# Fewer VectorE operations for products and weighted values, and input rows in the value projections' tile

## The chip, the cores and the metric

The kernel runs on one core of a Trainium2 chip. The metric is the device time of one execution in microseconds. The core's engines are TensorE (PE in the profile, its weight loads PEld), VectorE (DVE), ScalarE (ACT), GpSimd (POOL) and SyncE (SP). POOL and SP also issue DMA transfers.

## The reference

Two branches read the same input `x` of 2048 rows and 640 columns, and a gate mixes them:

```python
g = _sigmoid((x * gate_w).sum(-1, keepdims=True))
a = _A_ref(x, A_wqkv, A_wo)        # 32 heads of 20, each row looks at 8 rows, 2 apart
b = _B_ref(x, B_A_re, ..., B_Dskip)
return g * a + (1 - g) * b

# A: sliding dilated attention
logits = jnp.einsum("bhsd,bhswd->bhsw", q, kg) * scale      # kg, vg: rows s, s-2, ..., s-14
attn = _softmax(logits, axis=-1)
o = jnp.einsum("bhsw,bhswd->bhsd", attn, vg)                # then o @ wo

# B: state space convolution
P = jnp.exp(logdA[:, :, None] * l[None, None, :])           # 640 x 192 x 2048, complex
K = jnp.einsum("dn,dnl,dn->dl", Cc, P, dB).real
y = irfft(rfft(u) * rfft(K))[:L] + u * Dskip
```

## The kernel before

The program has a main stage and a tail. The main stage runs the attention and builds the convolution kernel `K` side by side; the tail does the convolution in the frequency domain, mixes and stores. In each stage, the work is a list of named tasks with an engine each. The order of the tasks is a table of numbers (`ORDER`), and every engine executes its tasks strictly in that order. A task that waits holds back everything behind it on its engine.

**Attention.** The projections of q, k and v (L284) are computed in four pieces of 512 rows into PSUM tiles `tb`, of which there are two, and copied out by ACT or DVE into `qr`, `kr` and, for v, into the tile `prj`. `prj` holds all four pieces of v. Each finished piece is stored to DRAM (`vS`, L313), and for each of eight blocks of 256 rows a window of it is loaded back as `vc` (L337), two loads per block into two buffers in turn. Per block, DVE forms the products `prod` of q and shifted k (L343, five operations), TensorE sums them over a head (`lg`), DVE takes the maxima (`mx`, `hi`, `lo`), TensorE subtracts them, ACT takes the exponentials, and the probabilities pass through DRAM to `asb`. Then DVE multiplies the windows of v with them (`pv`, L417, five operations of 128x2048 a block), TensorE sums (`tb`, L424), and the output projection follows (L448).

**Convolution kernel.** `K` is built in ten chunks of three units. For a unit, ACT writes sines (L784, `trg`) and exponentials (L786, `exq`) into rings of slots in the tiles `big` and `bufA`. A slot has 32 groups; a group of `trg` has 32 sines and twice 21 sines, and a group of `exq` has 32 and 21 exponentials. DVE multiplies them in three operations (L806 twice with 1024 elements, the second with the sines read backwards, and L808 with 1344) into `pt` and `qq`, and TensorE contracts these in 64 or 128 small matrix products (L824, `kps`). The tasks are `pq`, `pqb`, `pqc` (DVE) and `kmm{chunk}{unit}{0..3}` (TensorE).

**Input rows.** The convolution needs `x` in another layout, `Usb` (128 x 64 x 160). It is loaded in eight pieces (`rows0` to `rows7`, L972) by POOL into the memory of `prj`, as a new tile in the same place, so the first load waits for the last store of `prj`. Ahead of each later piece, POOL copies two elements of the one before (`pace`, L971), which makes POOL wait until that piece has landed. `Usb` is read by the matrix products of L1276 at the end of the main stage.

## Time and profile before

| | |
|---|---|
| median of three runs | 325.98 us (324.89 to 327.3) |
| profiled execution | 324.97 us, its span 323.2 us |
| DVE busy | 294.0 us, 91% of the span, 408 instructions |
| ACT busy | 281.5 us, 87% |
| PE busy | 278.4 us, 86% |
| POOL busy | 62.8 us, 19% |
| chain that ended last | PE 48%, ACT 39%, issue 5%, DVE 3% |
| tail (from about 254 us) | about 69 us |

A busy share says how much an engine did, not who held up whom. The chain of waits is followed back from the last instruction; it says which work the end actually hung on. Both are read together with the table of idle times and what ended them.

### The profile page before, as it was taken

To read this page: it belongs to the slowest core of one execution; us is meant where nothing else is said; L and a number is where in the kernel's file an instruction comes from. 1 tells how busy PE (TensorE), PEld (TensorE's weight loads), DVE (VectorE), ACT (ScalarE), POOL (GpSimd) and SP (SyncE) were. 2 spreads that over 40 slices of the span, in tenths; PEclk is the share of its full clock that TensorE was granted. 3 is DMA by queue.
4 is the path that set the end of the run, shared out by engine and by line. 5 is a ranking of instruction groups with operands and counts; after the bars stand their busy time and mean duration, and the time that the engine had idled before them with its cause. 6 is when DMAs were issued, how large, how long until landed. Compare 5 with 4: busy or idle time off the path is not lost.

```text
span 323.2 us, 11733 instructions
## 1 busy us (share of the span) xinstructions
PE 278.4 (86%) x5109; PEld 170.3 (53%) x5134; DVE 294.0 (91%) x408; ACT 281.5 (87%) x425; POOL 62.8 (19%) x94
## 2 busy tenths in 40 slices
PE   0599997999979999999998979889999999997750
PEld 0145543444545645546554545457678776657740
DVE  4888999899998999999999989898998999999891
ACT  1479678999989999999999999899988599996991
POOL 8500026501100000111134523320200000000063
PEclk9999999999999999999999997999999999997995
DMA  8997356662414102467774996533860593962057
GB/s 213 338 227 224 122 173 138 130 128 83 92 30 109 37 6 74 81 161 254 179 190 97 161 179 141 108 96 77 254 258 33 151 312 95 204 123 44 2 135 194
DMA packets 48697, 45.65 MB, mean 141 GB/s; under 512 B 28590, under 2 KB 42482, under 8 KB 48646
## 3 DMA queue, kind: packets, MB, share of 16 engines
q1 hardware_dynamic: 42524, 27.82, 33.7%
q0 software_dynamic: 5216, 16.39, 20.8%
q8 instruction: 40, 0.66, 0.9%
q10 hardware_dynamic: 906, 0.69, 0.7%
q14 instruction: 11, 0.09, 0.1%
HBM read 28.25 MB, written 14.01 MB: 131 GB/s over the span
## 4 chain that ended last, share of the span: by engine, by line
PE 48%; ACT 39%; issue 5%; DVE 3%; SPq 2%; DMA 2%; POOL 0%; POOLq 0%; ACTq 0%; DVEq 0%
PE tb L284 14%; ACT big L784 8%; PE fp L1043 7%; PE ar L769 7%; ACT big L786 6%; PE kps L824 5%; ACT bufA L476 4%; PE tb L424 4%; PE tb L448 4%; ACT L160 3%; PE bp L1276 3%; ACT tt L1140 2%; ACT bufA L784 2%; ACT sp_k L476 2%; DMA bufA<-in_A_wqkv_dram 2%
## 5 line engine op out<-in xcount | busy, mean ns | idle before, releaser
L284 PE MATMUL tb<-bufA 128*128 128x512 bf16 x275 | 73.4, 394 | 6.5 <-DMA bufA<-in_A_wqkv_dram 2.9
L784 ACT ACTIVATE big<-ar 128x740 bf16<-128x740 int16 (+1 forms) x72 | 56.1, 849 | 2.4 <-PE ar L769 1.9
L786 ACT ACTIVATE big<-ar 128x848 bf16<-128x848 f32 x60 | 50.4, 919 | 3.2 <-PE ar L769 3.0
L769 PE MATMUL ar<-Rarg,L 64*128 64x212 bf16 (+4 forms) x600 | 47.1, 253 | 6.3 <-ACT big L784 2.5
L284 PEld LDWEIGHTS <-bufA 128*128 128x128 bf16 x300 | 32.3, 121 | 35.2 <-issue 12.0
L417 DVE TENSOR_TENSOR pv<-vc,asb 128x2048 bf16<-128x2048 bf16 x40 | 47.6, 1217 | 1.1 <-DMA vc<-vS 0.9
L343 DVE TENSOR_TENSOR prod<-qr,kr 128x2048 bf16<-128x2048 bf16 x40 | 47.8, 1218 | 0.5 <-PE lg L349 0.5
L769 PEld LDWEIGHTS <-L 64*128 64x128 bf16 x600 | 22.3, 95 | 35.0 <-issue 32.1
L806 DVE TENSOR_TENSOR pt<-big 128x1024 bf16<-128x1024 bf16 x48 | 32.1, 701 | 1.5 <-PE kps L824 0.8
L824 PE MATMUL kps<-qq,pt 128*32 128x21 bf16 (+1 forms) x2560 | 28.1, 175 | 3.3 <-issue 3.1
L824 PEld LDWEIGHTS <-pt 128*32 128x32 bf16 (+1 forms) x2560 | 23.4, 91 | 12.2 <-issue 10.1
L448 PE MATMUL tb<-wo_sb,oTm 128*128 128x320 bf16 x160 | 27.1, 300 | 0.1
L337 POOL DMA_DIRECT2D vc<-vS x16 | 11.5, 727 | 70.6 <-DVE pv L417 65.4
L476 ACT ACTIVATE sp_u<-fp 128x640 bf16<-128x640 f32 x29 | 22.4, 883 | 2.1 <-PE fp L1043 2.1
L476 ACT ACTIVATE sp_k<-fp 128x640 bf16<-128x640 f32 x30 | 22.7, 878 | 1.0 <-PE fp L1043 0.8
L424 PE MATMUL tb<-pv,ind 128*64 128x512 bf16 (+1 forms) x192 | 22.7, 359 | 0.3 <-ACT qr L476 0.2
L808 DVE TENSOR_TENSOR qq<-big 128x1344 bf16<-128x1344 bf16 x24 | 21.2, 884 | 0.0
L1043 PEld LDWEIGHTS <-PHI 128*128 128x128 bf16 x160 | 15.6, 97 | 8.1 <-issue 1.5
L1161 POOL DMA_DIRECT2D out_dram<-ot x14 | 7.8, 562 | 54.9 <-DVE ot L1143 54.9
L448 PEld LDWEIGHTS <-oTm 128*128 128x128 bf16 x160 | 14.5, 98 | 7.3 <-issue 2.7
L160 ACT ACT_TABLE_LOAD x14 | 18.0, 1283 | 0.3
L476 ACT ACTIVATE qr<-tb 128x512 bf16<-128x512 f32 (+1 forms) x22 | 10.8, 514 | 6.7 <-PE tb L284 6.7
(153 smaller groups left out, 512.0 us busy)
## 6 DMA issues: line engine op xcount, KB each, us to landing
vc<-vS POOLq DMA_DIRECT2D x16, 327.5 KB, 5.8
vS<-prj POOLq DMA_DIRECT2D x4, 640.0 KB, 5.7
gaS<-ga SPq DMA_DIRECT2D x8, 320.0 KB
Usb<-in_A_x_dram POOLq DMA_DIRECT2D x8, 320.0 KB, 5.0
gaF<-gaS SPq DMA_DIRECT2D x8, 320.0 KB
bufA<-in_A_wqkv_dram SPq DMA_DIRECT2D x3, 800.0 KB
Sprm<-pc SPq DMA_DIRECT2D x10, 240.0 KB
L<-Sprm SPq DMA_DIRECT2D x38, 60.0 KB
```

The costliest lines, as they stand in the source:

```text
L284: nc.tensor.matmul(ppf, self.wq[:, which, kt, e::5], self.xT[:, c0 // 1024, kt, c0 % 1024:c0 % 1024 + SC], start=(kt == 0), stop=(kt == NK ...
L343: nc.vector.tensor_tensor(b[e][:], self.qr[:, sc % NRB, e, :].unsqueeze(1).to_broadcast([128, W, C]), win(self.kr[:, sc % NRB, e, :], 0, W ...
L417: nc.vector.tensor_tensor(o, vw, b["asb"][:].unsqueeze(2).to_broadcast(sh), ALU.mult)
L424: nc.tensor.matmul(b["op", e][64 * a:64 * a + 64, 0:n, :], ind[:, 32:96], b["pv", e][:, w, a, 0:n, :], start=(w == 0), stop=(w == 3), skip ...
L448: nc.tensor.matmul(apf[:, :320], b["oT"][:, e, i * 128:(i + 1) * 128], wo_sb[:, e, hf * 320:(hf + 1) * 320], start=(e == 0), stop=(e == 4))
L476: nc.scalar.activation(o, i, ACT.Identity)
L769: nc.tensor.matmul(ar[:, g2, a0:a0 + ncol], L[rows, gv, sb, l0:l0 + 128], R[rows, c0:c0 + ncol], start=True, stop=True, tile_position=(64 ...
L784: nc.scalar.activation(d_[:, :, s0 * QW:s1 * QW], ar[:].bitcast(I16)[:, :, 0:2 * (s1 - s0) * QW:2], ACT.Sin, scale=SCL)
L786: nc.scalar.activation(dst[:, gp::2].rearrange("p g s n -> p g (s n)"), ar[:, :, 0:2 * EW], ACT.Exp)
L806: nc.vector.tensor_tensor(pt[:, :, k, :], gg[:, :, ::-1] if k else gg, e1, ALU.mult)
L824: nc.tensor.matmul(kps[32 * g:32 * g + 32, h ^ (g // 2), NM * ql:NM * ql + NM], pt[rows, k, v, :], qq[rows, k, v, :], start=(g not in star ...
L1043: nc.tensor.matmul(fp[:, fl % 2, 0:320].rearrange("p (c x) -> p c x", x=32), phis[fb][:, fl, kind, :], B[:, :, 2 * f1 + ri].rearrange("p c ...
```

## The change

Three things are changed.

1. **Products.** The constant table behind the sines is laid out anew, so that a group of `trg` reads: 21 sines of the second kind reversed, 32 sines, 21 sines of the first kind. One slice of 53 sines, read forwards from element 21 or backwards from element 52, then meets the 53 exponentials of a group, and two operations of 32 x 53 elements write what `pt` and `qq` held, side by side in one tile `pq`. The task `pqc` is gone; `pq` and `pqb` are longer. TensorE reads its operands from `pq`.
2. **Weighted values.** `vS` is laid out as 64 x 5 x 2 x rows, so that the windows of four rows of v lie one after another in `vc`, and one operation of 128x4096 takes the place of two of 128x2048. A block has three operations instead of five. Each store of `prj` to `vS` becomes two stores.
3. **Input rows.** `Usb` is now a view of the tile `prj` itself. Pieces 0 to 3 lie where the first two pieces of v were, and follow the first two stores only; pieces 4 to 7 follow all stores. The copies `pace` are gone. Instead each load waits for a task of TensorE named in `TICKS`.

```diff
+TICKS = ("kmm120", "kmm220", "kmm320", "kmm420", "kmm600", "kmm620", "kmm710", "kmm720")
...
-    "560 -1 -541 1 28 1 1 163 -124 1 1 123 -152 1 140 -139 37D 114 1 1 -152 139 14 1 -153 1 186 2 -178 1 1 141 1 393 -559 "
+    "544 -1 -525 1 28 1 1 163 -124 1 1 123 -152 1 140 -139 37D 114 1 1 -152 139 14 1 -153 1 184 2 -176 1 1 141 1 374 -540 "
...
-        self.vS = dr.tile([128, 5, HALO + S], BF16, name="vS")
+        self.vS = dr.tile([64, 5, 2, HALO + S], BF16, name="vS")
...
             def store(_, c0=c0, sc=sc):
-                nc.gpsimd.dma_start(self.vS[:, :, HALO + c0:HALO + c0 + SC], open_()[:, sc])
+                for a in range(2):
+                    nc.gpsimd.dma_start(self.vS[:, :, a, HALO + c0:HALO + c0 + SC], open_()[a::2, sc])
...
-                    sh, step, o = ([128, 4, 2, C], VW, b["pv", e][:, :, k]) if n == 2 else ([128, 4, 2, C], 5 * VW, b["pv", e][:, :, :, 0])
-                    vw = bass.AP(vt[:].tensor, vt[:, k, e, :].offset, [list(vt[:].ap[0]), [DIL, 4], [step, 2], [1, C]])
-                    nc.vector.tensor_tensor(o, vw, b["asb"][:].unsqueeze(2).to_broadcast(sh), ALU.mult)
+                    vw = bass.AP(vt[:].tensor, vt[:, e, 0, :].offset, [list(vt[:].ap[0]), [DIL, 4], [VW, 2 * n], [1, C]])
+                    nc.vector.tensor_tensor(b["pv", e][:, :, 0:2 * n], vw, b["asb"][:].unsqueeze(2).to_broadcast([128, 4, 2 * n, C]), ALU.mult)
...
-    rr = np.concatenate([np.concatenate([p, q.reshape(64, 4, -1)], axis=2).reshape(64, -1) for p, q in ((sp, sq), (ep, eq))], axis=1)
+    rr = np.concatenate([np.concatenate([sq[:, :, 1, ::-1], sp, sq[:, :, 0]], axis=2).reshape(64, -1), np.concatenate([ep, eq], axis=2).reshape(64, -1)], axis=1)
...
-                        b["pq", u] = self.tb.tile([128, 32, 2, KI], BF16, name="pt"), self.tb.tile([128, 32, 2, NM], BF16, name="qq")
-                    pt, qq = b["pq", u]
-                    if k < 2:
-                        nc.vector.tensor_tensor(pt[:, :, k, :], gg[:, :, ::-1] if k else gg, e1, ALU.mult)
-                    else:
-                        nc.vector.tensor_tensor(qq[:], trg[:, :, KI:].rearrange("p a (v m) -> p a v m", v=2),
-                                                exq[:, :, KI:].unsqueeze(2).to_broadcast([128, 32, 2, NM]), ALU.mult)
+                        b["pq", u] = self.tb.tile([128, 32, 2, KI + NM], BF16, name="pq")
+                    nc.vector.tensor_tensor(b["pq", u][:, :, k, :], trg[:, :, KI + NM - 1::-1] if k else trg[:, :, NM:], exq, ALU.mult)
...
-                                                     pt[rows, k, v, :], qq[rows, k, v, :],
+                                                     pq[rows, k, v, 0:KI], pq[rows, k, v, KI:],
...
-        g, h = n // 2, n % 2
+        g, h = n % 4, n // 4
         if n == 0:
-            P["Usb"] = pre.tile([128, 64, 160], BF16, name="Usb", tag="uga")
-        else:
-            g0, h0 = (n - 1) // 2, (n - 1) % 2
-            nc.gpsimd.tensor_copy(P["pace"][32 * g0:32 * g0 + 32, :], P["Usb"][32 * g0:32 * g0 + 32, 32 * h0, 0:2])
+            P["Usb"] = P["prj"]()[:].rearrange("p a e s -> p (a e s)").rearrange("p (b d) -> p b d", d=160)
...
-            ub.append(pl.add(f"rows{n}", "G", 1.4 if n else 0.7, lambda _, n=n: rows(n), deps=ub[-1:], after=list(at.stored.values()), dma=2.0))
+        ticks = {t.name: t for t in pl.tasks}
+        for n, tick in enumerate(TICKS):
+            ub.append(pl.add(f"rows{n}", "G", 0.7, lambda _, n=n: rows(n), deps=[ticks[tick]], after=ub[-1:] + [v for k, v in at.stored.items() if k < 2 or n >= 4], dma=2.0))
+            ub[-1].waits = [ticks[tick]]
```

On PE, ACT and SP the tasks stand in the same order as before. On DVE the removed operations are left out and the others keep their order. On POOL the row loads move.

The first place is DVE where the first weighted values and the first units of products are made, at 60.8 to 72 us of the trace. `prod` and `pv` are the products of the attention, `mx`, `hi`, `lo` the maxima, `kr<-tb` the copy of a projection out of PSUM. Before:

```order
L806 TENSOR_TENSOR pt<-big 128x32x32 x2
L343 TENSOR_TENSOR prod<-qr,kr 128x2048
L808 TENSOR_TENSOR qq<-big 128x1344
L343 TENSOR_TENSOR prod<-qr,kr 128x2048 x2
L417 TENSOR_TENSOR pv<-vc,asb 128x4x512
L365 TENSOR_REDUCE mx<-lg 128x64
L368 TENSOR_SCALAR hi<-mx 128x64
L369 SCALAR_TENSOR_TENSOR lo<-mx,hi 128x64
L806 TENSOR_TENSOR pt<-big 128x32x32 x2
L478 CAST kr<-tb 128x2x256
L417 TENSOR_TENSOR pv<-vc,asb 128x4x512
L808 TENSOR_TENSOR qq<-big 128x1344
```

And now:

```order
L802 TENSOR_TENSOR pq<-big 128x32x53 x2
L345 TENSOR_TENSOR prod<-qr,kr 128x2048 x3
L418 TENSOR_TENSOR pv<-vc,asb 128x4096
L367 TENSOR_REDUCE mx<-lg 128x64
L370 TENSOR_SCALAR hi<-mx 128x64
L371 SCALAR_TENSOR_TENSOR lo<-mx,hi 128x64
L802 TENSOR_TENSOR pq<-big 128x32x53 x2
L477 CAST kr<-tb 128x2x256
```

The second `pv` and the `qq` that stood behind the copy `kr<-tb` are now done in the longer operations ahead of the maxima and of the copy.

The second place is POOL from the store of v's second piece to the window loads for blocks 4 to 6. `vS<-prj` is a store of v, `vc<-vS` the window loads (two per block), `Usb` and later `prj<-in_A_x_dram` the row loads, `Kx<-X` and `kc<-Kx` the convolution kernel on its way through DRAM. Before, up to the fourth row load:

```order
L313 DMA vS<-prj 640x1x512
L337 DMA vc<-vS 64x10x262 x4
L313 DMA vS<-prj 640x1x512
L898 DMA Kx<-X 64x4x640
L313 DMA vS<-prj 640x1x512
L972 DMA Usb<-in_A_x_dram 32x32x160
L907 DMA kc<-Kx 128x2560
L971 COPY pace<-Usb 32x2
```

And now, the whole stretch:

```order
L315 DMA vS<-prj 320x1x512 x2
L339 DMA vc<-vS 64x10x262 x2
L960 DMA prj<-in_A_x_dram 32x32x160 x3
L339 DMA vc<-vS 64x10x262 x2
L315 DMA vS<-prj 320x1x512 x2
L960 DMA prj<-in_A_x_dram 32x32x160
L890 DMA Kx<-X 64x4x640
L315 DMA vS<-prj 320x1x512 x2
L899 DMA kc<-Kx 128x2560
L960 DMA prj<-in_A_x_dram 32x32x160 x2
L339 DMA vc<-vS 64x10x262 x4
L960 DMA prj<-in_A_x_dram 32x32x160 x2
```

Four row loads now stand ahead of the last store of v. Two more stand ahead of the window loads for blocks 4 and 5, which before stood behind the fourth and the fifth row load and their copies.

## Prediction

> **What bounds the kernel now.** I read the page first: the busy times and the chain that ended last.

> ```profile
> span 323.2 us, 11733 instructions
> ```
> ```profile
> PE 278.4 (86%) x5109; PEld 170.3 (53%) x5134; DVE 294.0 (91%) x408; ACT 281.5 (87%) x425; POOL 62.8 (19%) x94
> ```
> ```profile
> PE 48%; ACT 39%; issue 5%; DVE 3%; SPq 2%; DMA 2%; POOL 0%; POOLq 0%; ACTq 0%; DVEq 0%
> PE tb L284 14%; ACT big L784 8%; PE fp L1043 7%; PE ar L769 7%; ACT big L786 6%; PE kps L824 5%; ACT bufA L476 4%; PE tb L424 4%; PE tb L448 4%; ACT L160 3%; PE bp L1276 3%; ACT tt L1140 2%; ACT bufA L784 2%; ACT sp_k L476 2%; DMA bufA<-in_A_wqkv_dram 2%
> ```

> DVE is the busiest engine, and the change takes work from it. Yet the chain runs over DVE for 3% of the span, some 9.7 us. Where those lie is told by the chain in order of time. It has eleven pieces on DVE; here are the first and the last:

> ```profile
> 247.54 0.56 DVE ga L459
> 314.75 1.07 DVE ot L1143 x2
> ```

> Ahead of 247.5 us the chain does not touch DVE at all, and `prod`, `pv` and the products of L806 and L808 all lie ahead of that. The busy times by stretch say who fills the main stage (from, to, length, then the busy us of PE, PEld, DVE, ACT and POOL with the number of instructions):

> ```profile
> 60.00:230.00 170.00, 157.16 (x3776) 90.77 (x3795) 161.98 (x231) 165.28 (x240) 30.71 (x42) 0.99 0.50 117
> 230.00:254.00 24.00, 23.57 (x191) 17.66 (x189) 22.39 (x25) 19.56 (x29) 2.18 (x4) 1.00 0.48 161
> ```

> From 60 to 230 us ACT works 165.28 of 170 us, 97%, against 95% for DVE and 92% for PE. From 230 to 254 us PE works 98%. Neither engine gets less work by the change. The longest entries of the table of idle times, ACT's and PE's for 60 to 230 us, then DVE's:

> ```profile
> ACT big L786 <- PE ar L769: 3.0, 3, 1.3
> ```
> ```profile
> PE kps L824 <- issue: 3.1, 4, 1.3
> ```
> ```profile
> DVE ga L459 <- PE tb L448: 1.2, 2, 1.0
> ```

> ACT waits for PE, PE for its own instructions, DVE for PE. DVE runs close behind no one: it is ahead and is waited for only in short spots. PE's weight loads name those:

> ```profile
> L824 PEld LDWEIGHTS <-pt 128*32 128x32 bf16 x1280 | 12.3, 93 | 5.8 <-issue 4.3 <-DVE prod L343 0.2 <-DVE pv L417 0.2
> L824 PEld LDWEIGHTS <-pt 64*32 64x32 bf16 x1280 | 11.1, 90 | 6.4 <-issue 5.9 <-DVE qq L808 0.2
> L424 PEld LDWEIGHTS <-ind 128*64 128x64 bf16 x192 | 9.6, 110 | 8.5 <-issue 4.3 <-DVE qq L808 0.2 <-DVE bufA L478 0.2
> ```

> Five times 0.2, that is 1.0 us, is all that DVE shows as a cause there.

> **Products.** The groups and two stretches of DVE's timeline:

> ```profile
> L417 DVE TENSOR_TENSOR pv<-vc,asb 128x2048 bf16<-128x2048 bf16 x40 | 47.6, 1217 | 1.1 <-DMA vc<-vS 0.9 <-PE tb L424 0.2
> L806 DVE TENSOR_TENSOR pt<-big 128x1024 bf16<-128x1024 bf16 x48 | 32.1, 701 | 1.5 <-PE kps L824 0.8 <-ACT big L784 0.4 <-ACT big L786 0.3
> L808 DVE TENSOR_TENSOR qq<-big 128x1344 bf16<-128x1344 bf16 x24 | 21.2, 884 | 0.0
> ```
> ```profile
> 60.83 1.32 DVE L806 TENSOR_TENSOR pt<-big 128x1024 bf16<-128x1024 bf16 x2
> 62.07 1.22 DVE L343 TENSOR_TENSOR prod<-qr,kr 128x2048 bf16<-128x2048 bf16 x1
> 63.21 0.88 DVE L808 TENSOR_TENSOR qq<-big 128x1344 bf16<-128x1344 bf16 x1
> 64.01 2.44 DVE L343 TENSOR_TENSOR prod<-qr,kr 128x2048 bf16<-128x2048 bf16 x2
> ```
> ```profile
> 66.37 1.22 DVE L417 TENSOR_TENSOR pv<-vc,asb 128x2048 bf16<-128x2048 bf16 x1
> 67.50 0.68 DVE L365 TENSOR_REDUCE mx<-lg 128x64 f32<-128x512 f32 x1
> ```

> Operations overlap by some 0.08 us, so I take the distance between starts. Two `pt` take 62.07 - 60.83 = 1.24, or 0.62 each for 1024 elements; `qq` takes 64.01 - 63.21 = 0.80 for 1344; `pv` takes 67.50 - 66.37 = 1.13 for 2048. A unit costs 1.24 + 0.80 = 2.04 us. From 1024 to 2048 elements the time grows by 0.51, 0.50 ns an element. A new operation has 32 x 53 = 1696 elements: from `pt` 0.62 + 672 x 0.0005 = 0.96, from `qq` 0.80 + 352 x 0.0005 = 0.98. I take 0.97, so 1.94 a unit, and 0.10 less than before. Bounds by proportion: from `pv` 1.13 x 1696/2048 = 0.94, from `qq` 0.80 x 1696/1344 = 1.01, a gain of 0.16 or 0.02 a unit. For ten chunks of three units: **3.0 us** of DVE (0.6 to 4.8). The elements are the same number; only one start per unit is saved.

> **Weighted values.** 4096 elements: twice 1.13 = 2.26 at most, 1.13 + 2048 x 0.0005 = 2.15 at least; I take the middle, 2.20. Sixteen pairs become one: 16 x 0.06 = **1.0 us** (0 to 1.8). With the products DVE loses 4.0 us of work (0.6 to 6.6).

> None of it lies on the chain. What it can reach is the 1.0 us in which PE is shown to wait for DVE. I book that as the gain, **-1.0**, from 0 up.

> **What is later.** DVE's copy of a projection out of PSUM, and what PE did next:

> ```profile
> 69.83 0.68 DVE L478 CAST kr<-tb 128x512 bf16<-128x512 f32 x1
> ```
> ```profile
> 71.80 1.25 PE L284 MATMUL tb<-bufA 128*128 128x512 bf16 x5
> ```

> The longer operations stand ahead of work that waited behind shorter ones. Ahead of `mx` at 67.50: two products +0.70, `qq` gone -0.80, `pv` +1.07, so it starts 0.97 later. Ahead of the copy `kr<-tb` at 69.83 two more products: +1.67. Its end moves from 70.51 to 72.18. There are two `tb`, and the projection at 71.80 takes the one that this copy empties; it comes 0.38 later. Everything on PE stands behind it. I book **+0.4**, 0 if PE's gaps take it up. No later copy is shifted by more than +0.3 (a unit and a block are mostly complete ahead of each), and they come earlier and earlier, by up to 4 us at the end.

> **Stores, row loads, windows.** POOL's timeline and the median landing of a window in us, the tile of the rows, the one wait of DVE for a window, and a piece of the chain of waits:

> ```profile
> 50.41 1.46 POOL L337 DMA_DIRECT2D vc<-vS  x2 [5.22 <-DMA vS<-prj]
> ...
> 178.41 1.43 POOL L337 DMA_DIRECT2D vc<-vS  x2
> ```
> ```profile
> vc<-vS POOLq DMA_DIRECT2D x16, 327.5 KB, 5.8
> ```
> ```profile
> L1276 PE MATMUL bp<-F1c,Usb x80: 269/272/348, 222.1 to 252.9; 128*128 128x256 bf16 x80
> L972 POOL DMA_DIRECT2D Usb<-in_A_x_dram x8: 787/792/820, 157.0 to 203.8; - x8
> ...
> DMA to landing us min/median/max: 4.7/5.0/7.5
> ```
> ```profile
> 187.04 2.36 DVE L417 TENSOR_TENSOR pv<-vc,asb 128x2048 bf16<-128x2048 bf16 x2 [0.87 <-DMA vc<-vS]
> ```
> ```profile
> 174.64 0.59 PE kps L824 x57
> ```

> A second store costs POOL one more issue, 0.8 us by the row loads' 792 ns, ahead of the window at 50.41. That window's first reader starts at 66.37, and windows land 5.8 us after issue, so it costs nothing: the cover is some 8 us, and whatever exceeded it would hold the first `pv`. The last row load is issued at 203.8 and lands by 211.3 at the latest; its first reader starts at 222.1. Loading earlier is therefore worth nothing in itself. The copies and their waits are on POOL, off the chain. The waits that are new are POOL's on TensorE. Queued behind the sixth row load is the window pair that DVE waited 0.87 us for. Its tick follows unit 2 of chunk 6, done near 174 us (the chain's `kps` work at 174.64), so the window leaves at about 175 and not at 178.4. That wait goes; it is DVE's and off the chain: **0**.

> **Sum.** -1.0 + 0.4 = -0.6. The profiled execution's own time is 324.97 (span 323.2 and 1.8 around it), so 324.4. It lay 1.0 below the median of the runs, 325.98; on that scale I forecast **325.4 us**.

> **The rivals.**

> *DVE is the pace after all.* It is the busiest engine, and idles in short waits that could close. Then the whole 4.0 and the 0.9 us wait come off: 325.98 - 4.9 = 321.1. For it: 91% busy, and the five waits of PE. Against it: no piece of the chain before 247 us. Chance 0.20.

> *Odd starts halve the rate.* The forward product reads its sines from element 21, and the second writes from element 53, both 2 bytes past a multiple of 4. If such an operation lost the fast rate, the price comes from float32 work of 960 elements:

> ```profile
> L593 DVE TENSOR_TENSOR wr<-wr,t 128x960 f32<-128x960 f32 x1 | 1.2, 1158 | 0.0
> ```

> That is 1.1 ns an element with the overlap taken off, so 1.9 us for 1696, 3.8 a unit and not 2.04: 30 x 1.76 = 53 more. DVE has 8 us of idle time from 60 to 230 us to take it up, so about 45 is left: 371. It decides at once, in every unit. Against it stand the two `pt` of one unit:

> ```profile
> 73.56 0.70 DVE L806 TENSOR_TENSOR pt<-big 128x1024 bf16<-128x1024 bf16 x1
> ...
> 76.45 0.70 DVE L806 TENSOR_TENSOR pt<-big 128x1024 bf16<-128x1024 bf16 x1
> ```

> The second reads its sines backwards from element 31, also 2 bytes off, and both take 0.70. No row has a forward read or a write from such a place. Chance 0.05. [...]

> *TensorE reads the shared tile slower.* Half of the weight loads in L824 now start at odd elements, in rows of 53 and not 32. The chain has `kps` work for 5% of the span, 16 us. If half of it took 1.7 times as long, 5.6 us: 331. For it: those loads are the smallest and most numerous on PE. Against it: the other operand, `qq`, has odd rows of 21 already, and the loads beside them keep 90 to 93 ns in both forms. Chance 0.07.

> *The rows arrive no earlier than before,* since a tick or a store holds POOL. With 222.1 - 211.3 = 10.8 us of slack this changes no time; it is part of the forecast.

> **How the numbers follow.** Forecast 0.68, with its own range from 324.0 (twice the booked gain, no loss) to 327.7 (no gain, the loss of 0.4, and the 1.3 by which the highest run lay above the median); rivals 0.20, 0.05 and 0.07. About 1%, 3.3 us, is what a measurement of this kernel can tell from no change. Faster: the first rival and a little of the forecast's edge, 0.22. Slower: the two others, 0.12. Same: 0.66. The range goes from just under the first rival, 320.9, to 327.7; the slower rivals stay out.

> **What would show it.** Right: `pq` near 1.05 us busy (0.97 and the overlap), the larger `pv` near 2.28, DVE 4 us less busy, ACT and PE as before, DVE's idle time up by some 4 us, the row loads from about 100 us on, no DVE in the chain ahead of 247 us. Wrong: a main stage that ends before 251 us with ACT and PE closing up, since then DVE was the pace; `pq` near 2 us; `kps` weight loads over 100 ns.

## The result and the profile after

The change made the kernel slower: **327.64 us** median of 20 runs (326.01 to 331.09) against 326.66 (323.35 to 331.58) for the kernel before beside it, a ratio of **1.0075** (95% interval 1.005 to 1.0101). The profiled execution took 327.13 us, its span 325.4. The forecast was 0.6 us faster. A few runs of each kernel are in a slower state; medians and ranges here are over all runs, ratios over the others.

What was costed by the piece came as costed. First the busy times of the page, then the groups of the new operations and of their weight loads:

```profile
PE 277.5 (85%) x5109; PEld 168.8 (52%) x5134; DVE 289.7 (89%) x362; ACT 281.6 (87%) x425; POOL 57.6 (18%) x91
```
```profile
L802 DVE TENSOR_TENSOR pq<-big 128x1696 bf16<-128x1696 bf16 x48 | 48.5, 1050 | 1.0 <-PE kps L817 0.8
L418 DVE TENSOR_TENSOR pv<-vc,asb 128x4096 bf16<-128x4096 bf16 x16 | 36.3, 2280 | 0.0
L817 PEld LDWEIGHTS <-pq 128*32 128x32 bf16 x1280 | 12.3, 94 | 5.4 <-issue 3.9 <-DMA L<-Sprm 0.2 <-DVE pv L418 0.2
L817 PEld LDWEIGHTS <-pq 64*32 64x32 bf16 x1280 | 11.2, 90 | 7.4 <-issue 7.2
```

`pq` takes 1050 ns and the large `pv` 2280, DVE has 4.3 us less to do (294.0 to 289.7), and TensorE's weight loads from the shared tile take 94 and 90 ns, where those from the two tiles took 93 and 90. So the loss is in no operation. It is in waits. The longest two of the main stage, in all, how often, and the longest one:

```profile
PE kps L817 <- issue: 4.0, 3, 2.0
ACT big L785 <- PE ar L768: 3.7, 2, 2.1
```

Before, these were 3.1 and 3.0 us, the longest 1.3 each. Where the time went is read from the starts of the same pieces of TensorE's work in both profiles (its order is the same):

| piece of TensorE's work | before | after | difference |
|---|---|---|---|
| `tb<-bufA`, a projection | 67.36 | 66.34 | -1.0 (the loads at the start) |
| `ar`, twenty microseconds later | 86.70 | 86.08 | -0.6 |
| `kps`, second half of a unit | 93.11 | 92.62 | -0.5 |
| `ar` | 97.48 | 98.05 | +0.6 |
| `ar` | 172.40 | 173.00 | +0.6 |
| `kps`, 48 products | 199.59 | 199.10 | -0.5 |
| `kps`, second half of a unit | 204.15 | 204.58 | +0.4 |
| `kps`, 128 products | 219.20 | 220.63 | +1.4 |
| `tb<-pv` of the last block | 240.43 | 242.57 | +2.1 |

From 100 to 173 us nine tenths of the differences lie between 0.57 and 0.61, although DVE does less work in every unit there: its saved time is worth nothing. The step back by 1.1 us after that is the kernel before's own: a gap of 0.58 us at 174 us and 3.41 us at a granted clock of 0.5 from 195.08 us, which this execution of the changed kernel did not have. The other steps lie at four places. TensorE's timeline shows them, of the changed kernel and then of the one before:

```profile
71.30 1.24 PE L285 MATMUL tb<-bufA 128*128 128x512 bf16 x5 [0.27 <-DVE kr L477]
...
90.77 0.36 PE L817 MATMUL kps<-pq 64*32 64x21 bf16 x30
92.62 0.39 PE L817 MATMUL kps<-pq 64*32 64x21 bf16 x34 [1.49 <-issue]
...
94.46 0.63 PE L375 MATMUL lg<-hi,ident 128*128 128x512 bf16 x1
...
204.58 0.42 PE L817 MATMUL kps<-pq 64*32 64x21 bf16 x37 [2.02 <-issue]
...
242.57 1.92 PE L425 MATMUL tb<-pv,ind 128*64 128x512 bf16 x16 [0.32 <-DVE ga L458]
```
```profile
91.47 0.36 PE L824 MATMUL kps<-qq,pt 64*32 64x21 bf16 x30
93.11 0.39 PE L824 MATMUL kps<-qq,pt 64*32 64x21 bf16 x34 [1.27 <-issue]
...
94.36 0.38 PE L373 MATMUL lg<-hi,ident 128*128 128x512 bf16 x1
...
204.15 0.42 PE L824 MATMUL kps<-qq,pt 64*32 64x21 bf16 x37 [1.10 <-issue]
```

At 71.30 and 242.57 us TensorE waits for a copy of DVE, which it did not before. The first step is 0.5 us, of which 0.24 is made up again by 76 us; the second is 0.34. In the middle of 64 small products TensorE stands still with "issue" as the cause: it waits for nothing that the profile shows, and the transfers below put it down to its next instructions. That gap existed, 1.27 us; it became 1.49, and behind it a product `lg` of the same size takes 0.63 us and not 0.38, in a stretch at half clock (0.51 from 93.1 to 96.5 us, where before it was 1.0). Of the 1.3 us lost there in this pair of executions, the longer gap is 0.2 and the slow stretch the rest. Near 203 us the same happens once more: the gap grows from 1.10 to 2.02 us, a stretch at half clock follows (0.5 from 205.78 to 209.19 us), and from 202 to 213 us this pair loses 1.9 us, its largest step. A shorter wait of the same kind near 223 us adds 0.3. The chain of waits of the kernel before had named the first gap:

```profile
91.84 1.27 issue
```

### The profile page after: what moved, and what is told of

Same layout as the page of the kernel before. It is cut to its first block, busy times and chain, and to the rows that moved or that the text cites. A ratio compares the mean times of both kernels' runs of the same rounds, so it can differ in the third digit from the quotient of the medians.

```text
span 325.4 us, 11686 instructions
## 1 busy us (share of the span) xinstructions
PE 277.5 (85%) x5109; PEld 168.8 (52%) x5134; DVE 289.7 (89%) x362; ACT 281.6 (87%) x425; POOL 57.6 (18%) x91
## 5 line engine op out<-in xcount | busy, mean ns | idle before, releaser
L285 PEld LDWEIGHTS <-bufA 128*128 128x128 bf16 x300 | 32.1, 121 | 35.1 <-issue 10.9
L802 DVE TENSOR_TENSOR pq<-big 128x1696 bf16<-128x1696 bf16 x48 | 48.5, 1050 | 1.0 <-PE kps L817 0.8
L345 DVE TENSOR_TENSOR prod<-qr,kr 128x2048 bf16<-128x2048 bf16 x40 | 47.7, 1217 | 0.7 <-PE lg L351 0.5
L418 DVE TENSOR_TENSOR pv<-vc,asb 128x4096 bf16<-128x4096 bf16 (+1 forms) x24 | 45.9, 1926 | 0.7 <-PE tb L425 0.7
L817 PE MATMUL kps<-pq 128*32 128x21 bf16 (+1 forms) x2560 | 28.0, 175 | 4.1 <-issue 4.0
L817 PEld LDWEIGHTS <-pq 128*32 128x32 bf16 (+1 forms) x2560 | 23.5, 92 | 12.8 <-issue 11.0
L447 PE MATMUL tb<-wo_sb,oTm 128*128 128x320 bf16 x160 | 28.4, 312 | 0.0
L425 PE MATMUL tb<-pv,ind 128*64 128x512 bf16 (+1 forms) x192 | 21.8, 349 | 0.9 <-ACT oTm L475 0.3
L960 POOL DMA_DIRECT2D prj<-in_A_x_dram x8 | 6.4, 803 | 73.2 <-PE kps L817 61.1
L475 ACT ACTIVATE big<-bp 128x1024 bf16<-128x1024 f32 x15 | 14.8, 1027 | 1.1 <-PE bp L1264 0.9
## 6 DMA issues: line engine op xcount, KB each, us to landing
vc<-vS POOLq DMA_DIRECT2D x16, 327.5 KB, 5.4
```

What stands on the lines that cost most here:

```text
L285: nc.tensor.matmul(ppf, self.wq[:, which, kt, e::5], self.xT[:, c0 // 1024, kt, c0 % 1024:c0 % 1024 + SC], start=(kt == 0), stop=(kt == NK ...
L345: nc.vector.tensor_tensor(b[e][:], self.qr[:, sc % NRB, e, :].unsqueeze(1).to_broadcast([128, W, C]), win(self.kr[:, sc % NRB, e, :], 0, W ...
L418: nc.vector.tensor_tensor(b["pv", e][:, :, 0:2 * n], vw, b["asb"][:].unsqueeze(2).to_broadcast([128, 4, 2 * n, C]), ALU.mult)
L425: nc.tensor.matmul(b["op", e][64 * a:64 * a + 64, 0:n, :], ind[:, 32:96], b["pv", e][:, w, a:2 * n:2, :], start=(w == 0), stop=(w == 3), s ...
L447: nc.tensor.matmul(apf[:, :320], b["oT"][:, e, i * 128:(i + 1) * 128], wo_sb[:, e, hf * 320:(hf + 1) * 320], start=(e == 0), stop=(e == 4))
L475: nc.scalar.activation(o, i, ACT.Identity)
```

## The experiments

All ratios are to the kernel before, with 95% intervals; each kernel ran beside it on the same chip.

### The parts alone

`p_only` has the products alone, `v_only` the weighted values with `vS` and its two stores, `r_only` the row loads, `pv_both` the first two.

```diff
 p_only:  -b["pq", u] = pt 32x2x32 and qq 32x2x21, three operations     +pq 32x2x53, two operations
 v_only:  -vS 128x5xrows, pv in halves of 128x2048                      +vS 64x5x2xrows, pv of 128x4096
 r_only:  -Usb as a new tile, behind all stores, with pace copies       +Usb a view of prj, TICKS
 pv_both: p_only and v_only
```

> The products alone are fused (two operations of 32x53 elements a unit, one tile for TensorE to read); weighted values and row loads as before. Theory S (longer operations stand ahead of the copy out of PSUM near 70 us): with the products alone that copy is 0.6 us later, less than its slack of 1.3 us, so no change, within 0.3%. Theory K (TensorE reads its operands slower from the joint tile, and its stalls on kps at 92 and 204 us grow): 0.5 to 1% slower, weight loads of kps above 92 ns or its idle time by 'issue' above 3.1 us. Theory R (the row loads): no change.

> The weighted values alone are fused (with the new layout of vS and two stores for each piece of v); products and row loads as before. Theory S: the copy near 70 us is 1.07 us later, still less than its slack of 1.3 us, so no change, within 0.3%. Theory K: no change. Theory R: no change. Slower by 0.5% or more would mean that the new layout or the second store costs by itself.

> The row loads alone are changed (view of the value projections' tile, waits on TensorE tasks, no copies on POOL); products and weighted values in their old operations. Theory S and theory K: no change, within 0.3%. Theory R (rows loaded from 94 to 140 us meet the transfers of that stretch or hold POOL's queue, and TensorE's own instructions come later): 0.5 to 1% slower, with more idle time by 'issue' on kps.

> Products and weighted values fused, the row loads as before. Theory S: the copy near 70 us is 1.67 us later, more than its slack of 1.3 us, and TensorE starts all that follows 0.4 us later: 0.1 to 0.2% slower. Theory K: as the products alone, 0.5 to 1% slower. Theory R: at most the 0.1% of theory S, so the whole change is not seen here.

| kernel | median us | ratio |
|---|---|---|
| p_only | 328.31 | 1.0057 (1.0004 to 1.0111) |
| v_only | 329.02 | 1.0046 (0.9992 to 1.01) |
| r_only | 326.0 | 1.0007 (0.9974 to 1.004) |
| pv_both | 327.71 | 1.0063 (1.0025 to 1.0101) |

The row loads are worth nothing, as forecast. The products alone lose, which the late copy at 70 us does not explain: by the starts of TensorE's work it costs nothing lasting with the products or the weighted values alone, and 0.5 us with both, of which half is made up again by 76 us. That is theory S, and it is too small. The waits of TensorE for DVE show a second place of the same kind, at 242 us, in the three kernels with the longer weighted values: a wait of 0.32 us. The gap near 91 us is 1.62 us in p_only and 1.49 in pv_both, each with the slow stretch behind it, and 1.08 and 0.77 in v_only and r_only, without. p_only's ratio lies in the range that K set, and its longer gap is one of K's signs; but the weight loads of the shared tile take 94 and 90 ns in it, against 93 and 90, so K's cause has no support. The profiled execution of v_only, at 329.75 us, has one wait of 3.27 us of DVE near 186 us that no other has and that shows no cause. The interval of v_only reaches below 1, and what it loses beyond those 0.3 us, if anything, isn't settled.

### The two copies, and TensorE's two gaps

`after_fix` is the whole change with DVE's order mended where TensorE waits for it:

```diff
 near 70 us          pq<-big (first)
-                    pq<-big (second)
                     kr<-tb
+                    pq<-big (second)
 last block, 242 us -pv 128x4096
+                    pv 128x2048
                     ga<-tb
+                    pv 128x2048
```

> The whole change, with VectorE's order mended at two places: the copy kr<-tb near 70.6 us goes ahead of the second product of its unit, and in the last block the large weighted-value operation is done in two halves again, with the copy ga<-tb between them (242 us). Theory S (longer operations stand ahead of two copies that TensorE waits for): the two waits of TensorE for VectorE, 0.27 us at 71.30 and 0.32 us at 242.57, are gone, and with them 0.4 + 0.34 = 0.7 us; ratio to the kernel before about 1.005 where the change has 1.0075. Theory G (the larger part of the loss is TensorE running out of instructions near 91 and 203 us and the half clock behind that): the 0.7 us comes off but 1.0 to 1.7 us stay. Rival N (the two waits were taken up elsewhere): still 1.0075.

`before_ns` and `after_ns` are the two kernels with another order on TensorE at two places, `after_fix_ns` has both mends:

```diff
 near 91 us   kps x64,  lg x8
+             ar x8,  tb<-bufA x2
              kps x64
-             ar x8,  tb<-bufA x2
 near 203 us  kps x32
+             ar x8,  tb<-wo_sb x5
              kps x64
-             ar x8,  tb<-wo_sb x5
```

> The kernel before, with some of TensorE's work put into its two runs of small products: near 91 us eight products of ar and two of tb go between the first and the second 64 products kps of a unit, and near 203 us eight products of ar and five of tb likewise. The same instructions, only their order on TensorE. Theory G: TensorE's instructions come in pieces of 256, some 2.6 us after their transfer starts, and small products use a piece up faster than that; with 1.0 us more work in the piece the gaps shrink from 1.27 to about 0.3 us at 91.8 and from 1.10 to about 0.1 us at 203, so 1 to 2 us less in the profile, and in the runs 0.3 to 0.6% less (ratio 0.994 to 0.997), half clock behind these two places included. Rival W (the gaps are waits for data, or are taken up by ACT, which is as busy): ratio 0.999 to 1.001.

> The whole change, with the same pieces of TensorE's work put into the two runs of small products, and nothing else. Theory G: the gaps of 1.49 us at 91.13 and 2.02 us at 202.55 shrink by 1.0 us each, no window of the clock there is idle enough for the half clock at 93.1 and 205.8, and 1.5 to 3 us come off: ratio 0.999 to 1.003. If G is the whole of the loss beyond the two copies, its distance to the kernel before with the same order is 0.7 us (0.2%). Rival C (the products in one tile cost TensorE or VectorE time of their own, outside the gaps): the distance to the kernel before with the same order stays at 0.75%. Rival W: still 1.0075.

> Both mends in the changed kernel: VectorE's order at two places, and TensorE's at two. Theories S and G together: 0.7 and 1.5 to 3 us less than the change, ratio to the kernel before 0.995 to 1.0005, and within 0.2% of the kernel before with TensorE's order mended. Rival C: 0.5% above that kernel. If VectorE's 4 us less work were worth anything once these waits are gone, it would be below that kernel.

| kernel | median us | ratio |
|---|---|---|
| after_fix | 327.79 | 1.0052 (1.0012 to 1.0091) |
| before_ns | 323.48 | 0.992 (0.9872 to 0.9968) |
| after_ns | 324.28 | 0.9945 (0.9908 to 0.9982) |
| after_fix_ns | 322.63 | 0.9914 (0.9883 to 0.9946) |

In after_fix both waits for DVE are gone from the timeline:

```profile
71.44 1.25 PE L287 MATMUL tb<-bufA 128*128 128x512 bf16 x5
...
242.46 1.97 PE L427 MATMUL tb<-pv,ind 128*64 128x512 bf16 x16
```

The ratio falls by 0.0023, 0.75 us, as S said (the intervals of 1.0075 and 1.0052 overlap; the rows are what shows it). The gaps were worth more than G expected: filling them takes 0.8% off the kernel before, and all three kernels with TensorE's order mended lie 0.2 to 0.45% below the ranges set for them. TensorE's timeline of before_ns near 91 us, where short waits for ACT are left:

```profile
92.15 0.62 PE L351 MATMUL lg<-prod,ind 128*32 128x512 bf16 x8
92.98 0.36 PE L771 MATMUL ar<-Rarg,L 64*128 64x212 bf16 x4 [0.21 <-ACT big L788]
93.75 0.36 PE L771 MATMUL ar<-Rarg,L 64*128 64x212 bf16 x4 [0.41 <-ACT big L788]
94.04 0.63 PE L286 MATMUL tb<-bufA 128*128 128x512 bf16 x2
94.60 0.65 PE L826 MATMUL kps<-qq,pt 64*32 64x21 bf16 x64
```

With the gaps filled, the change is 0.25% above before_ns (0.9945 and 0.992), about the 0.7 us of the two copies; with these mended as well it is level (0.9914). Rival C asked for 0.75% and 0.5%. Each of these ratios has an interval of 0.3 to 0.5% to either side, so one comparison alone would not refute it; both together speak against it, and for the gaps as the place of the rest of the loss. What is left to explain is why the change makes a gap longer in which TensorE's work is the same.

### What TensorE's instructions wait for

The trace holds the transfers of TensorE's own instructions: pieces of 16384 bytes on queue q8, 40 for the 10,243 weight loads and products of the page, on average one for 256. In every profile that has it, the gap near 91 us ends 2.6 to 3.0 us after its piece starts to move; and the 127 weight loads before it take 3.15 to 3.17 us in every kernel with TensorE's order untouched. So the gap is the longer, the later the piece (0.96 to 2.05 us in the table below). The queue's row of the changed kernel:

```profile
q8 instruction: 40, 0.66, 0.8%
```

The DMA engines by stretch show what ran ahead of it. First the changed kernel (from, to, length; the last two numbers are the busy share of the DMA engines and GB/s), then the piece:

```profile
87.80:89.75 1.95, 1.77 (x46) 1.05 (x49) 1.95 (x3) 1.93 (x3) 0.00 (x0) 1.00 1.01 204
89.75:91.10 1.35, 1.35 (x102) 0.83 (x98) 0.76 (x2) 1.34 (x3) 0.00 (x0) 1.00 0.06 9
91.10:92.60 1.50, 0.03 (x5) 0.00 (x0) 1.43 (x4) 0.66 (x1) 0.00 (x0) 1.00 0.00 0
```
```profile
q8 instruction: 1, 0.02, 6.2%
```

That last row is the same queue from 89.7 to 91.1 us: one piece. From 87.80 to 89.75 the 16 engines are full, at a busy share of 1.01; then the piece moves. What fills them is the window load `vc<-vS` of block 2 (97% of the engines' time in that stretch is its queue), which POOL issues as soon as block 0's last weighted values are done. POOL's timeline of the changed kernel, and DVE's of it and of the kernel before:

```profile
85.16 1.44 POOL L339 DMA_DIRECT2D vc<-vS  x2 [8.58 <-DVE pv L418]
```
```profile
81.31 2.02 DVE L802 TENSOR_TENSOR pq<-big 128x1696 bf16<-128x1696 bf16 x2 [0.40 <-PE kps L817]
83.24 0.49 DVE L477 CAST E<-kps 128x336 bf16<-128x336 f32 x1
83.66 1.21 DVE L418 TENSOR_TENSOR pv<-vc,asb 128x2048 bf16<-128x2048 bf16 x1
```
```profile
82.06 1.33 DVE L806 TENSOR_TENSOR pt<-big 128x1024 bf16<-128x1024 bf16 x2 [0.40 <-PE kps L824]
...
83.72 1.22 DVE L417 TENSOR_TENSOR pv<-vc,asb 128x2048 bf16<-128x2048 bf16 x1
84.86 0.68 DVE L478 CAST qr<-tb 128x512 bf16<-128x512 f32 x1
85.46 0.88 DVE L808 TENSOR_TENSOR qq<-big 128x1344 bf16<-128x1344 bf16 x1
```

The products start as soon as TensorE's `kps` lets them. Before, two short ones stood ahead of `pv`, which starts 1.66 us after them, and `qq` stood behind it. Now two long ones stand ahead, and it starts 2.35 us after them. `pv` and the window load behind it come that much later against the products. Theory V says that TensorE's piece of instructions has to wait for this load. If so, it is the same fault as at the two copies, two hand-overs further on. Three kernels test it by moving this `pv` alone (before_late moves `qq` ahead of it):

```diff
 before_late:                before_early:                after_early (on after_fix):
  pt<-big x2                 +pv                          +pv
 +qq<-big                     pt<-big x2                   pq<-big x2
  E<-kps                      E<-kps                       E<-kps
  pv                         -pv                          -pv
 -qq<-big
```

> The kernel before, with one move on VectorE: the product qq<-big that stood behind the last weighted values of the first block (pv, 83.72 us) goes ahead of them, so that this pv comes 0.8 us later against TensorE; in the changed kernel the two longer products ahead of it make it 0.65 us later. Theory V (this pv frees the window buffer; the window load vc<-vS that follows keeps the DMA engines full, and TensorE's next piece of instructions only starts when it is through): the load ends 0.8 us later, the gap of TensorE at 91.8 us grows from 1.27 us (0.8 to 1.3 in the three kernels with unchanged products) to 1.6 to 2.0, the window of the clock is idle enough for the half clock near 93 to 95 us, and the ratio is 1.003 to 1.005. Rival A (the gap's length is chance, or comes from the products in one tile): gap 0.8 to 1.3 us, ratio 0.999 to 1.001.

> The kernel before, with the last weighted values of the first block (pv, 83.72 us) moved ahead of the two products at 82.06 us, so that they come 2.3 us earlier or less. Theory V: the window load is through before TensorE's piece of instructions is due, the piece starts at once, and the gap at 91.8 us falls from 1.27 us to at most 0.4; ratio 0.996 to 0.998. Rival A: gap 0.8 to 1.3 us, ratio 0.999 to 1.001.

> The changed kernel with VectorE's order mended at the first two places (ratio 1.0052), and the last weighted values of the first block moved ahead of the two products as well. TensorE's order is untouched. Theory V: the gap at 91.1 us falls from 1.7 us to at most 0.4, no half clock follows at 93 us, and 1.2 to 2.5 us come off: ratio to the kernel before 0.998 to 1.0015. Rival A: 1.004 to 1.006, gap still 1.5 to 1.7 us.

From the traces, one execution each. All times but the gap count from one mark, the start of the first weight load of the 64 products of `kps` ahead of those with the gap (89.64 us in the change, 90.35 before):

| kernel | `pv` starts ahead of the mark | window load through | piece starts, is through | gap between weight loads | ratio |
|---|---|---|---|---|---|
| before | 6.63 us | +0.12 | +0.12, +1.34 | 1.46 us | 1 |
| r_only | 6.63 | +0.02 | -0.36, +0.99 | 0.96 | 1.0007 |
| v_only | 6.63 | +0.22 | -0.15, +1.12 | 1.28 | 1.0046 |
| p_only | 5.98 | +0.78 | +0.53, +1.84 | 1.82 | 1.0057 |
| pv_both | 5.99 | +0.80 | -0.01, +1.42 | 1.68 | 1.0063 |
| after | 5.98 | +0.74 | +0.11, +1.50 | 1.68 | 1.0075 |
| after_fix | 5.99 | +0.80 | +0.48, +1.77 | 1.86 | 1.0052 |
| before_late | 5.98 | +0.70 | +0.69, +1.90 | 2.05 | 1.0 (0.9955 to 1.0045) |
| before_early | 8.76 | -1.91 | -1.19, -0.23 | 0.00 | 0.9968 (0.9934 to 1.0002) |
| after_early | 8.76 | -2.20 | -1.57, -0.64 | 0.00 | 1.0013 (0.9977 to 1.0049) |

The gap follows the time at which the piece is through, and ends 1.3 to 1.6 us behind it. The piece does not simply start when the load ends: in the change it starts 0.6 us before that, no later than in the kernel before (+0.11 and +0.12), and is through 0.16 us later. So in this one pair the later load explains a gap that is 0.2 us longer, and no more.

before_late has the old products and the new gap, with the slow stretch behind it; before_early has no gap. Their rows of TensorE, and the piece of before_early, which moved between 87.7 and 89.6 us:

```profile
90.93 0.36 PE L826 MATMUL kps<-qq,pt 64*32 64x21 bf16 x30
93.15 0.39 PE L826 MATMUL kps<-qq,pt 64*32 64x21 bf16 x34 [1.85 <-issue]
...
95.07 0.63 PE L375 MATMUL lg<-hi,ident 128*128 128x512 bf16 x1
```
```profile
90.17 0.61 PE L351 MATMUL lg<-prod,ind 128*32 128x512 bf16 x8
90.72 0.65 PE L826 MATMUL kps<-qq,pt 64*32 64x21 bf16 x64
91.30 0.83 PE L771 MATMUL ar<-Rarg,L 64*128 64x212 bf16 x8
```
```profile
q8 instruction: 1, 0.02, 3.2%
```

What theory V expects of the gap is shown by the rows in both directions: with the load through 1.91 us ahead of the mark there is no gap, with the load through 0.70 us behind it and unchanged products it is 2.05 us and not 1.46. The times are weaker. after_early is 0.39% below after_fix, 1.3 us, and before_early 0.3% below before, but the intervals of the first two overlap and that of before_early reaches 1. The time of before_late decides nothing: its runs reach from 322.34 to 329.82 us, and its interval holds most of what V expected and all of what A did. Rival A falls on the gap alone, which is 2.05 us with unchanged products. Clear of noise is the sum: after_early differs from the change in VectorE's work at three places only (two operations moved, one split around a copy), and takes the ratio from 1.0075 (1.005 to 1.0101) to 1.0013 (0.9977 to 1.0049).

The last kernel is after_early with TensorE's order mended near 203 us as well, as in before_ns:

```diff
 after_early_ns203:  after_early, and near 203 us  kps x32  +ar x8  +tb<-wo_sb x5  kps x64
```

> The changed kernel with all the mends that each took a loss away: VectorE's order at the two copies, the last weighted values of the first block ahead of the two products (so that TensorE's piece of instructions is there in time near 91 us), and near 203 us eight products of ar and five of tb between the small products of a unit, as before. Near 91 us TensorE's order is untouched, where the kernel with TensorE's order mended at both places let TensorE wait 0.4 us for ACT. If the two gaps and the two copies are all that the change can lose, and VectorE's 4 us less work are worth nothing: the gap at 91 us stays 0, that at 203 us is at most 0.7 us, and the ratio to the kernel before is 0.988 to 0.992, level with both kernels with TensorE's order mended (0.9914 and 0.992). If something of the change's loss is still hidden: 0.993 to 0.997.

Measured: **322.27 us** (321.7 to 323.2), ratio **0.9924** (0.9899 to 0.995), between the two ranges expected (0.988 to 0.992 if nothing is hidden, 0.993 to 0.997 if something is), so that it does not decide between them by itself; it is level with before_ns (0.992). Its waits of TensorE for its own instructions and of ACT for TensorE, which were 4.0 and 3.7 us in the change:

```profile
PE kps L822 <- issue: 1.0, 2, 0.7
ACT big L788 <- PE ar L773: 1.7, 2, 1.5
```

This and after_fix_ns (0.9914) are faster than both kernels, by what the gaps were worth, and not by DVE's saved work.

## Why the prediction was wrong

**Right.** The sizes: 0.97 us a product and 2.20 a pair by start distances, and 4.3 us less DVE where 4.0 were forecast. The odd starts: all 60 products ran in 1050 ns, with a read from element 21 or a write from element 53, where the rival asked for near 2 us. The shared tile: 94 and 90 ns, under the 100 that I named. The row loads: no time (1.0007), the first issued at 99 us. "None of it lies on the chain": kernels with 4 us less DVE work are level with kernels without, once the waits are gone. The +0.4 of the copy `kr<-tb` arrived at 71.3 us as 0.5; gaps of TensorE took up 0.24 of it by 76 us, a way out that the prediction had named.

**The booked gain of 1.0 us did not come.** I took five waits of 0.2 us of the weight loads for DVE as time that TensorE loses. These weight loads idled while the products flowed: from 100 to 173 us nine tenths of TensorE's starts stayed within 0.04 us. Such a row prices nothing unless the product behind it is late.

**"No later copy is shifted by more than +0.3".** I followed one copy and closed the rest with a rule about whole units and blocks. The copy `ga<-tb` near 242 us stood between the two halves of a `pv`, and the fused one put 1.13 us ahead of it; 0.34 us arrived at TensorE.

**"Stores, row loads, windows: 0" is the step that failed by most.** I asked when the window is read (8 us later) and found cover. I did not ask what the transfer stands ahead of. The window load of block 2 is through 0.6 us later against TensorE, and the piece with TensorE's next instructions is through 0.16 us later. By the ratios of the mended kernels the change's 0.75% divides into 0.23% for the two copies and 0.39% for this; 0.13%, 0.4 us, is left. Only the sum of the first two is clear of the intervals; how it divides is an estimate. "issue 5%" stood in the chain that I quoted, 16 us, more than DVE's 3%, and I priced none of it: I named the wait of TensorE for its own instructions and did not ask what sets its length. What such a gap costs is in part luck: it also depends on where it falls on the steps of the clock (last section), and these lie elsewhere in the two profiles: one starts at 92.68 us before (30 steps ahead of its half clock at 195.08) and at 93.14 in the change.

**The rivals.** DVE as the pace (0.20) is refuted, as are the odd starts and the slow shared tile. The case that came, slower by a transfer ahead of instructions, was not among them, though its measured size, 0.75%, lies inside what I called no change, and 327.64 inside the range.

**Open.** The gap near 203 us is 1.83 to 2.21 us in the four kernels with the new row loads and the old order on TensorE (r_only, after, after_fix, after_early), and 0.46 to 1.43 in five with the old row loads (before, p_only, pv_both, before_late, before_early). But v_only has the old row loads too, and 1.94. And r_only lost nothing, and after_early is level with the kernel before although its gap is the longest, 2.21. So the largest step of the profiled pair has no shown cause, and what it costs across executions isn't settled.

## What to carry to other kernels

When short operations are fused, list for each fused one what stood between its parts and right behind the first, follow each to the engine that waits, and follow a freed buffer through the transfer that it starts to what is transferred behind it. If a run of small matrix products shows "issue" as the cause of its wait, look at the transfers of its instructions; here the gap followed them (0.96 us with the piece through at +0.99, 2.05 with +1.90), and it helped to put slower work among the products (ratio 0.992), or to move the large transfer that stood ahead of them (no gap; 1.0013 and not 1.0052, with intervals that overlap). Here the engine that is busiest by share had 4.3 us less to do for nothing, and delays of 0.5 and 0.34 us at two copies and of 0.6 us at one window load went with a loss of 0.75%.

## What the runs showed of the hardware

**The gap follows the transfer of TensorE's instructions.** In the eight profiles of the table that have a gap, the piece of instructions starts between 0.8 us before the load ahead of it is through and the moment it is, and the gap ends 2.6 to 3.0 us after the start. With the load 2 us earlier, the piece starts 1.2 and 1.6 us ahead of the mark and there is no gap. 128 small products of one unit, 256 instructions with their weight loads, take TensorE 1.18 us (at 220.63 us of the change). There are gaps of 0.5 to 2.2 us at the same two places in all profiles with TensorE's order untouched there, but for those in which the window load was moved away from the first.

**A gap can be paid twice.** The granted clock after the gap of 1.49 us, of the changed kernel (the clock is the third number from the end):

```profile
93.10:96.50 3.40, 3.05 (x20) 1.19 (x18) 3.40 (x4) 2.60 (x4) 0.00 (x0) 0.51 0.02 5
```
